# Reordering the gather stage of a spectral-mixing and expert kernel: one-hots, one gather, one spectrum load and one turn

## The chip, the cores and the metric

The kernel runs on one core of one Trainium2 chip. The metric is the device time of one execution in microseconds (us), lower is better. Before the change it is 474.11 us, the median of three runs (473.17 to 475.94).

The core has a matrix engine (TensorE, "PE" in the profile, with its weight loads as "PEld"), a vector engine (VectorE, "DVE"), an activation engine (ScalarE, "ACT"), GpSimd ("POOL") and a queue engine (SyncE, "SP"). DMA transfers are issued by SP, ACT and POOL and run beside them. Each engine works through its own list of instructions in order and waits on semaphores for the others.

## The reference

Two steps. The first mixes each of 8 sequences of 2496 rows and 256 channels by multiplying its spectrum with a filter:

```python
X = np.fft.rfft(x, axis=1)
Y = X * (filt_r + 1j * filt_i)[None, :, :]
y = np.fft.irfft(Y, n=x.shape[1], axis=1)
```

The second treats the 19968 rows of `y` as tokens of a mixture of 8 experts with 80 places each. A token goes to its best expert; an expert that has more than 80 tokens keeps those with the largest gate; all other rows of the output are zero:

```python
logits = x @ w_gate
expert_idx = np.argmax(logits, axis=1)
gate_w = softmax(logits)[np.arange(N), expert_idx]
for e in range(E):
    tok_idx = the (at most capacity) tokens of e with the largest gate_w
    h = np.maximum(x[tok_idx] @ w1[e], 0.0)
    out[tok_idx] = gate_w[tok_idx, None] * (h @ w2[e])
```

Only 640 of the 19968 rows are needed after the choice, so the kernel never transforms back a whole sequence. It keeps the filtered spectra, computes the logits from them, chooses the rows, and transforms back only the chosen rows.

## The kernel before, in words

All instructions stand in an order written by hand (`manual_schedule`, from L782). The framework adds the waits on semaphores that the data needs; it moves nothing.

**Main loop (L853 to L896).** It runs over 80 pairs (sequence b, slice u) and two more turns of the loop. For each pair TensorE does a part of the forward transform (`stage1`, `transpose1`, `stage2`), VectorE multiplies by the filter (L339), GpSimd combines the products (L345), and `turn(b, u)` (L349) brings the result back into row order with four matrix products (L354). `turn` lags two behind, so the last one, `turn(7, 9)`, stands at loop value 81. ScalarE copies its result out, and every second turn it stores a piece of the spectrum `yf[b]` to memory. The table `early` (L836) hangs the choice of rows for the first three sequences (the early round, `pick_...` with round 0) between the turns of the loop. `pick_full(0, 0, NE)` (L683) is a check of that round that feeds only a flag for a rarely needed second path; it reads the PSUM tile `misc`.

**Row gathers and tiles.** For each sequence t there is a tile of up to 128 chosen rows. `fetch(t)` (L465) issues on GpSimd an indirect DMA that gathers 128 rows of 2560 numbers (10 KB each, 1.3 MB in all) from a table of inverse-transform coefficients, by the row numbers in `idxb[:, t]`. Two tiles share a buffer `gts`. `spectrum(t)` (L473) loads the filtered spectrum of sequence t, 2560 KB, on SP's queue; tiles 0 and 1 find it in SBUF already, the others have three buffers in turn (`ypool` twice, `st["yx"]` for t = 2 and 5). `turn_rows(t, g)` (L481) transposes a fifth of the gathered rows (TensorE L485, ScalarE copy L489 into `wt`). `add_rows(t, g)` (L491) multiplies it with the spectrum (L496). The result of a tile goes to `y_sel` in memory.

The list `work` (L901 to L907) holds these two steps in order, with the transposes two steps ahead of the products. Tiles 0 to 2 are one group and tiles 3 to 7 the next. `go(n)` (L910) emits the next n steps. After the last step of tile t, `go` emits `spectrum(t + 3)`; so spectrum 5 follows tile 2. After the last transposes of tile 3 it emits `fetch(6)` and `fetch(7)`.

**The late round (L946 to L975).** Between the steps of tiles 0 to 2 the rows of sequences 3 to 7 are chosen. `pick_slots(0)` makes the first slot of each partition. `pick_rows(1, NE, B, 5)` and part 6 (L666 to L681) make the row numbers `idxb` with small products and four VectorE operations, and `fetch(3)` follows (NE is 3). `pick_slots(1)` makes a table `eval` on GpSimd (L743). `fetch(4)` follows. `pick_slots(3)` makes the one-hots `eplc` of the slots on VectorE (L736). `pick_slots(2)` joins the two tables on TensorE (L750) after tile 2 and yields the indices of the experts' tokens. Then `gather_gates` issues eight small gathers on GpSimd (L223), `fetch(5)` follows, and tiles 3 to 7 run. `mark` is a tile of one number, written once near the start (L816) by a GpSimd copy of one loaded element; the copy makes GpSimd wait for that load.

**Experts (L977 to the end).** Gathers of the experts' rows from `y_sel`, two layers for each of eight experts, and scatters of the results.

Of the kernel before, what the change touches and what calls it, by code (L numbers as in the profile page):

```python
# [13 lines left out]
F32 = mybir.dt.float32  # L14
# [9 lines left out]
B, S, C = 8, 2496, 256  # L24
# [3 lines left out]
NU = NS // 2  # L28
# [53 lines left out]
def kernel(  # L82
# [11 lines left out]
    nc = tc.nc  # L94
# [13 lines left out]
    consts = ctx.enter_context(tc.tile_pool(name="consts", bufs=1))  # L108
# [70 lines left out]
    NE, NY, NO = 3, 2, 3  # L179
    yf = {b: dpool.tile([128, NS, C], F32, name=f"yf_{b}") for b in range(B)}  # L180
# [51 lines left out]
    with ExitStack() as actx:  # L232
        bctx = ExitStack()

        def pool(name, bufs, space=None, within=actx):
            kw = {} if space is None else {"space": space}
            return within.enter_context(tc.tile_pool(name=name, bufs=bufs, **kw))
# [9 lines left out]
        tpool = pool("tables", 1, within=bctx)  # L247
# [25 lines left out]
        def sign_filter(v):  # L273
            f = fst[:, v]
            for i in range(2):
                nc.scalar.activation(out=f[:, 2 + i, :], in_=f[:, 2 + i, :], func=AF.Copy,
                                     scale=fsig[:, 2 * v + i:2 * v + i + 1])
# [185 lines left out]
        wts, gts, ybs, pos = {}, {}, {}, {}  # L463

        def fetch(t):  # L465
            if t % 2 == 0:
                gts[t // 2] = t1pool.tile([128, 2, NS * 128], F32, name=f"gts_{t}", tag="t1")
            nc.gpsimd.indirect_dma_start(
                out=gts[t // 2][:, t % 2, :], out_offset=None, in_=rows[:, :],
                in_offset=bass.IndirectOffsetOnAxis(ap=idxb[:, t:t + 1], axis=0),  # L470
                bounds_check=S - 1, oob_is_err=False)

        def spectrum(t):  # L473
            p = ypool if t % NE < NE - 1 else st["yx"]
            ybs[t] = p.tile([128, NS, C], F32, name=f"yb_{t}", tag="ys")
            nc.sync.dma_start(out=ybs[t], in_=yf[t])

        def weights(e, p, tag, queue=nc.sync):
            load_weights(e, p.tile([128, 2 * NFC * C], F32, name=f"w_{e}", tag=tag), queue)
# [28 lines left out]
        def pt(shape, dt, name, rnd):  # L508
            return sp.tile(shape, dt, name=f"{name}_{rnd}", tag=name)
# [173 lines left out]
        def pick_full(rnd, b0, nb):  # L683
            if rnd == 0:
                nc.vector.tensor_scalar(out=viol[:, 4:5], in0=st["rcnt"][:], scalar1=float(K0),
                                        scalar2=None, op0=AL.is_gt)
            vb = pt([128, B], F32, "vb", rnd)
            nc.vector.tensor_scalar(
                out=vb[:, b0:nb], in0=st["poff"][:, 1, b0:nb], scalar1=128.0, scalar2=None,
                op0=AL.is_gt, op1=AL.add, accum_out=viol[:, 2 + 3 * (1 - rnd):3 + 3 * (1 - rnd)])  # L690
# [91 lines left out]
        with tc.manual_schedule():  # L782
# [29 lines left out]
                nc.gpsimd.memset(t[:], 0.0)  # L812
            nc.gpsimd.tensor_copy(out=gi[:, 0, E:E + 128], in_=ident[:])
            nc.gpsimd.tensor_copy(out=gi[:, 1, 0:128], in_=ident[:])
            mark = tpool.tile([1, 1], F32, name="mark")
            nc.gpsimd.tensor_copy(out=mark[:], in_=st["x", 0, NCH - 1][0:1, 0, 0:1])  # L816
            load_filter(1, 0)
            nc.gpsimd.dma_start(out=gi[:, 0, 0:E], in_=moe_w_gate[0:128, :])
# [11 lines left out]
            for v in range(LEAD):  # L830
# [8 lines left out]
                     71: [lambda: pick_misc(0), lambda: pick_tau(0), lambda: pick_kept(0, 0, NE)],  # L839
                     72: [lambda: pick_sums(0, 0, NE), lambda: pick_codes(0, 0, NE)],  # L840
                     73: [lambda: pick_fields(0), lambda: pick_rows(0, 0, NE, 0),
                          lambda: pick_rows(0, 0, NE, 1), lambda: pick_full(0, 0, NE)],
                     74: [lambda: pick_rows(0, 0, NE, 2), lambda: pick_rows(0, 0, NE, 3)],
                     75: [lambda: pick_rows(0, 0, NE, 4)],
                     76: [lambda: pick_rows(0, 0, NE, 5), lambda: pick_rows(0, 0, NE, 6),
                          lambda: fetch(0)],
                     79: [lambda: fetch(1)]}
            tops = [lambda i=i: pick_top(0, i, n0, 128) for i in range(n0)]
            third = -(-n0 // 3)
            early[68] += tops[:third]  # L850
# [2 lines left out]
            for v in range(B * NU + LATE):  # L853
                b, u = divmod(v, NU)
                if b < B:
                    stage2(b, u)
                    if v + 2 < NU:
                        if v % 2 == 1:
                            sign_filter(v // 2 + 1)
                        turn_filter(v // 2 + 1, v % 2)  # L860
                    if v < 4:
                        load_filter(3 + v // 2, v % 2)
                    elif v == 4:
                        nc.gpsimd.dma_start(out=e_t, in_=e_dram.ap())
                        nc.gpsimd.dma_start(out=wi_t, in_=wi_dram.ap())
                    w = v + LEAD
                    if w < B * NU:
                        transpose1(*divmod(w, NU))
                    put_s1()
                    if u == 3:  # L870
                        put_s1()
                    if b > 0:
                        put_zeros(1)
                if v >= LATE:
                    turn(*divmod(v - LATE, NU))
                if b > 0 and u == LATE:
                    logits(b - 1, 0)
                if b > 0 and b % 2 == 0:
                    if u == LATE + 1:
                        logits(b - 1, 1)  # L880
                    if b < 6 and u in (4, 5, 6, 7, 8, 9):
                        gating(b // 2 - 1, u - 4)
                        if u == 9:
                            gating(b // 2 - 1, 6)
                    elif b == 6 and u in (4, 5):
                        gating(2, 2 * u - 8)
                        gating(2, 2 * u - 7)
                    elif b == 6 and u in (6, 7):
                        gating(2, u - 2)
                        if u == 7:  # L890
                            gating(2, 6)
                for act in early.pop(v, []):
                    act()
                if v == B * NU:
                    turn_rows(0, 0)
                    turn_rows(0, 1)  # L896
            assert not (xs or s1 or early)
# [12 lines left out]
            def go(n):  # L910
                for kind, t, g in work[:n]:
                    if kind == "t":
                        turn_rows(t, g)
                        if g == NS // SG - 1 and t == NE:
                            fetch(6)
                            fetch(7)
                    else:
                        add_rows(t, g)
                        if g < NS // SG - 1:
                            continue  # L920
                        if t + 3 < B:
                            spectrum(t + 3)
                        if t == 4:
                            weights(0, wpool, "w")
                            weights(1, wpool, "w")
                del work[:n]
# [30 lines left out]
            for part in range(5):  # L957
                pick_rows(1, NE, B, part)
            pick_slots(0)
            go(FG[4])  # L960
            pick_rows(1, NE, B, 5)
            pick_rows(1, NE, B, 6)
            fetch(NE)
            pick_slots(1)
            fetch(NE + 1)
            pick_slots(3)
            go(FG[5])
            pick_full(1, NE, B)
            pick_bad()
# [583 lines left out]
```

## Time and profile before

| what | us |
|---|---|
| median of three runs | 474.11 |
| profiled execution, whole | 481.94 |
| profiled execution, span from first to last instruction | 480.1 |
| last matrix products of the main loop (L354) start | 299.31 |
| tile 0 starts (L485) | 298.38 |
| tile 3 starts | 338.00 |
| tile 4 starts | 348.76 |
| last product of tile 7 (L496) | about 396.2 |
| experts' first product (L1115) | 400.08 |

Durations and starts are of the profiled execution, counted from its first instruction. A line of the timeline gives the start, the duration, the engine, the source line and operation, what is written and read, how many instructions are merged, and in brackets how long the engine had been idle and what ended that. A matrix product of 4-byte numbers shows as two records for each weight load and product, so four products are "x8". The waits view lists the idle time of an engine by what ended it: total, number of times, longest. The view of stretches lists for each engine its busy time and number of instructions, in the order PE, PEld, DVE, ACT, POOL, then the granted TensorE clock (1.00 is full), the DMA share and the GB/s moved.

### The profile page before, as it was taken

Reading aid. Unit: us, or ns where it says so; the run is one execution under the profiler, and the core shown is the slowest. Engines: PE = TensorE matmul, PEld = TensorE weight load, DVE = VectorE, ACT = ScalarE, POOL = GpSimd, SP = SyncE. Lnnn points to the kernel's source line nnn. Section 1 sums busy time; section 2 is a strip of 40 time slices with the busy share of each in tenths; the row PEclk is TensorE's granted clock in tenths of the full one; section 3 lists DMA queues with packets and bytes.
Section 4 is the critical chain, followed back from the end, with each engine's and each line's share of the span. In section 5 each row is a group of like instructions: output and inputs, shape, how many; then the busy total and the mean of one; then the engine's idle time right before and its main releaser. Section 6 shows DMA issues by size and latency. Waiting matters only on the chain. (4 is left out here: it accounts for less than half of the span.)

```text
span 480.1 us, 8658 instructions
## 1 busy us (share of the span) xinstructions
PE 442.1 (92%) x3372; PEld 416.0 (87%) x3372; DVE 187.9 (39%) x562; ACT 222.4 (46%) x364; POOL 176.6 (37%) x244
## 2 busy tenths in 40 slices
PE   5869999999999999999999987999889996999990
PEld 5769999999999999999999887888778886888870
DVE  2135553554664455655546995484110000011100
ACT  3835667666766666676667443322123220011110
POOL 7486434443543443444435446103620010211210
PEclk9979999999999999999999999999899996699996
DMA  7995467888778878788961326888779999155000
GB/s 215 279 293 167 151 192 218 246 262 251 250 247 254 268 271 248 203 265 280 401 238 47 132 89 213 311 338 324 283 268 383 379 389 349 53 181 173 20 18 11
DMA packets 38324, 109.95 MB, mean 229 GB/s; under 512 B 4667, under 2 KB 14202, under 8 KB 36760
## 3 DMA queue, kind: packets, MB, share of 16 engines
q1 hardware_dynamic: 26224, 73.26, 46.5%
q10 hardware_dynamic: 8642, 24.19, 13.1%
q0 software_dynamic: 3408, 11.86, 7.4%
q8 instruction: 29, 0.48, 0.4%
q14 instruction: 21, 0.17, 0.1%
HBM read 68.97 MB, written 43.20 MB: 234 GB/s over the span
## 5 line engine op out<-in xcount | busy, mean ns | idle before, releaser
L345 POOL TENSOR_TENSOR p<-p,p 128x256 f32<-128x256 f32 x160 | 114.0, 735 | 139.0 <-DVE p L339 97.2
L339 DVE TENSOR_TENSOR p<-pb,ft 128x512 f32<-128x512 f32 x160 | 102.3, 681 | 13.1 <-PE pb L331 10.7
L306 PE MATMUL pa<-wf_t,x 117*128 117x120 f32 x704 | 93.3, 280 | 6.6 <-DMA x<-in_x_dram 6.6
L312 ACT COPY t<-pa 128x480 f32<-128x480 f32 x88 | 87.0, 1000 | 26.4 <-PE pa L306 26.0
L306 PEld LDWEIGHTS pa<-wf_t,x 117*128 117x128 f32 x704 | 87.4, 197 | 6.9 <-DMA x<-in_x_dram 5.8
L354 PE MATMUL py<-gi,p 128*128 128x136 f32 x640 | 88.1, 280 | 1.3 <-POOL p L345 1.3
L331 PE MATMUL pb<-d_t,t 128*128 128x128 f32 x640 | 86.1, 278 | 0.9 <-DVE p L339 0.8
L354 PEld LDWEIGHTS py<-gi,p 128*128 128x128 f32 x640 | 79.8, 190 | 1.9 <-POOL p L345 1.9
L331 PEld LDWEIGHTS pb<-d_t,t 128*128 128x128 f32 x640 | 78.9, 193 | 1.7 <-DVE p L339 1.0
L322 ACT COPY t<-pt 128x512 f32<-128x512 f32 x80 | 46.9, 586 | 69.4 <-PE pt L320 64.8
L496 PE MATMUL po<-yb,wt 128*128 128x256 f32 x240 | 57.3, 383 | 2.0 <-ACT wt L489 2.0
L496 PEld LDWEIGHTS po<-yb,wt 128*128 128x128 f32 x240 | 43.8, 192 | 7.4 <-ACT wt L489 2.5
L320 PE MATMUL pt<-ident,t 128*128 128x128 f32 x320 | 48.5, 274 | 0.0
L489 ACT COPY wt<-pw 128x512 f32<-128x512 f32 x40 | 23.3, 586 | 54.1 <-PE pw L485 52.4
L374 DVE COPY z<-py 128x16 f32<-128x16 f32 x60 | 11.2, 186 | 91.9 <-ACT ysp L369 57.9
L320 PEld LDWEIGHTS pt<-ident,t 128*128 128x128 f32 x320 | 38.1, 143 | 0.0
L369 ACT COPY ysp<-py 128x512 f32<-128x512 f32 x60 | 35.4, 590 | 0.0
L1129 PEld LDWEIGHTS ph<-xs,w 128*128 128x128 f32 x256 | 32.9, 209 | 1.7 <-DVE xs L1120 1.2
L1129 PE MATMUL ph<-xs,w 128*128 128x80 f32 x256 | 33.1, 293 | 0.8 <-DVE xs L1120 0.8
L1144 PE MATMUL po<-w,hT 128*80 128x256 f32 x128 | 31.2, 402 | 0.0
L485 PE MATMUL pw<-ident,gts 128*128 128x128 f32 x160 | 24.7, 281 | 4.6 <-DMA gts<-rows_tbl,idxb 4.6
L1099 POOL DMA_INDIRECT xg<-y_sel,idxg x8 | 7.7, 962 | 55.9 <-ACT wt L489 40.3
(195 smaller groups left out, 315.7 us busy)
## 6 DMA issues: line engine op xcount, KB each, us to landing
out_dram<-zero_t SPq DMA_DIRECT2D x64, 312.0 KB
x<-in_x_dram SPq DMA_DIRECT2D x40, 468.0 KB
yf<-ysp ACTq DMA_DIRECT2D x30, 512.0 KB
yb<-yf SPq DMA_DIRECT2D x6, 2560.0 KB
w<-in_moe_w_dram SPq DMA_DIRECT2D x14, 1024.0 KB
yf<-ys ACTq DMA_DIRECT2D x10, 512.0 KB
w<-in_moe_w_dram ACTq DMA_DIRECT2D x2, 1024.0 KB
x<-in_x_dram SPq DMA_DIRECT2D x8, 234.0 KB
```

What stands on the lines that cost most here:

```text
L306: nc.tensor.matmul(out=ps[:, i, :, 2 * NS * cb:2 * NS * cb + 2 * NS], lhsT=xt[0:NJ * N1, (2 * k + i) % JC, 128 * cb:128 * cb + 128], rhs=w ...
L312: nc.scalar.copy(out=t1[:, 2 * k - h:2 * k - h + 2], in_=ps[:])
L320: nc.tensor.transpose(ps[:, i, cb, :], t1[:, a:a + 2, :].rearrange("p r n -> p (r n)"), ident[:])
L322: nc.scalar.copy(out=t2[:].rearrange("p i c -> p (i c)"), in_=ps[:].rearrange("p i c q -> p (i c q)"))
L331: nc.tensor.matmul(out=ps[:, cb, i], rhs=d_t[:, 2 * u + i, :], start=True, stop=True, lhsT=t2[:, i, 128 * cb:128 * cb + 128])
L339: nc.vector.tensor_tensor(out=pt, in0=ps[:].rearrange("p c s r q -> p (c s) r q"), in1=f.unsqueeze(2).to_broadcast([128, 2 * NDB, 2, NQ]), ...
L345: nc.gpsimd.tensor_tensor(out=yt[:, :, r, :], in0=yt[:, :, r, :], in1=pr[1][:, :, 1 - r, :], op=op)
L354: nc.tensor.matmul(out=ps[:, i, ZW * cb:ZW * cb + ZW], rhs=gi[:, cb, :], lhsT=yt[:, 2 * cb + i].rearrange("p r q -> p (r q)"), start=True, ...
L369: nc.scalar.copy(out=dst, in_=ps[:, :, E:E + C])
L496: nc.tensor.matmul(pos[t][:, 0, 0:C], lhsT=wts[t, g // 2][:, g % 2, i, :], rhs=ybs[t][:, s, :], start=(s == 0), stop=(s == NS - 1))
L1129: nc.tensor.matmul(ph[:, fc // 4, fc % 4, 0:cap], lhsT=self.w1s[e][:, k, 128 * fc:128 * fc + 128], rhs=xs[:, k, :], start=(k == 0), stop=( ...
L1144: nc.tensor.matmul(po[0:cap, :], lhsT=hT[:, fc, :], rhs=self.w2s[e][:, fc, :], start=(fc == 0), stop=(fc == NFC - 1))
```

## The change

Five edits, all in the order of instructions:

1. The first two `turn_rows` of tile 0 move from loop value 80 to 81, behind `turn(7, 9)`. TensorE now does the last turn and then the transposes, and ScalarE copies the turn's result out, issues its store, and then copies the transposes.
2. `pick_full(0, 0, NE)` moves from loop value 73 to 81. On VectorE its two operations now stand behind the last turn's addition.
3. `pick_slots(3)` moves ahead of parts 5 and 6 of `pick_rows`. On VectorE the one-hots `eplc` stand before the four operations that make `idxb`.
4. A GpSimd copy of one element of the gathered rows of tile 3 into `mark` stands before `fetch(4)`. GpSimd waits there until gather 3 has landed. The tile `mark` moves to a pool that lives to the end.
5. `spectrum(5)` is no longer issued by SP after tile 2. ScalarE issues it after its copy of the second transposes of tile 3. SP's list is one transfer shorter and otherwise the same.

```diff
-        def spectrum(t):
+        def spectrum(t, queue=nc.sync):
...
-            nc.sync.dma_start(out=ybs[t], in_=yf[t])
+            queue.dma_start(out=ybs[t], in_=yf[t])
...
-            mark = tpool.tile([1, 1], F32, name="mark")
+            mark = consts.tile([1, 1], F32, name="mark")
...
                      73: [lambda: pick_fields(0), lambda: pick_rows(0, 0, NE, 0),
-                          lambda: pick_rows(0, 0, NE, 1), lambda: pick_full(0, 0, NE)],
+                          lambda: pick_rows(0, 0, NE, 1)],
...
-                     79: [lambda: fetch(1)]}
+                     79: [lambda: fetch(1)],
+                     81: [lambda: pick_full(0, 0, NE)]}
...
-                if v == B * NU:
+                if v == B * NU + 1:
                     turn_rows(0, 0)
                     turn_rows(0, 1)
...
+                        if (t, g) == (NE, 1):
+                            spectrum(NE + 2, nc.scalar)
                     else:
                         add_rows(t, g)
...
-                        if t + 3 < B:
+                        if t + 3 < B and t != NE - 1:
                             spectrum(t + 3)
...
             pick_slots(0)
+            pick_slots(3)
             go(FG[4])
             pick_rows(1, NE, B, 5)
             pick_rows(1, NE, B, 6)
             fetch(NE)
             pick_slots(1)
+            nc.gpsimd.tensor_copy(out=mark[:], in_=gts[NE // 2][0:1, NE % 2, 0:1])
             fetch(NE + 1)
-            pick_slots(3)
             go(FG[5])
```

## The prediction

> **What bounds the kernel now.** I read the page's busy times first, then the waits of TensorE, then the timeline around each wait, then stretches of 1 us for clock and DMA.
>
> ```profile
> PE 442.1 (92%) x3372; PEld 416.0 (87%) x3372; DVE 187.9 (39%) x562; ACT 222.4 (46%) x364; POOL 176.6 (37%) x244
> ```
>
> TensorE works 92% of the span, so time is won only where it stands still. The waits view, filtered to TensorE (us in total, times, longest), says where:
>
> ```profile
> PE pa L306 <- DMA x<-in_x_dram: 6.6, 3, 5.8
> PE pf L284 <- ACT fst L276: 4.8, 4, 3.5
> PE pw L485 <- DMA gts<-rows_tbl,idxb: 4.6, 2, 2.4
> PE px L1115 <- DMA xg<-y_sel,idxg: 3.9, 1, 3.9
> PE po L496 <- ACT wt L489: 2.0, 1, 2.0
> ```
>
> The first two are the start of the kernel, which the change leaves alone. The third is two waits for gathered rows: 2.40 us before tile 0 and 2.25 us before tile 3. These the change is about. The timeline (start, duration, engine, line, idle time before and its releaser) at tile 0:
>
> ```profile
> 298.38 1.09 PE L485 MATMUL pw<-ident,gts 128*128 128x128 f32 x8 [2.40 <-DMA gts<-rows_tbl,idxb]
> 299.08 1.07 ACT L489 COPY wt<-pw 128x512 f32<-128x512 f32 x2 [2.39 <-PE pw L485]
> 299.21 1.00 PEld L354 LDWEIGHTS py<-gi,p 128*128 128x128 f32 x8
> 299.31 1.09 PE L354 MATMUL py<-gi,p 128*128 128x136 f32 x8
> 300.13 1.60 PEld L496 LDWEIGHTS po<-ys,wt 128*128 128x128 f32 x8
> ```
>
> The last turn (L354) sits behind the gather's wait although its input was ready: GpSimd's last products end at 291.95 + 4.15 = 296.10. At tile 3:
>
> ```profile
> 327.49 1.49 DVE L736 TENSOR_TENSOR eplc<-slot,iota 128x1280 bf16<-128x1280 f32 x1
> 327.85 2.00 POOL L468 DMA_INDIRECT gts<-rows_tbl,idxb  x1 [18.03 <-DVE idxb L681]
> ...
> 331.52 1.03 POOL L468 DMA_INDIRECT gts<-rows_tbl,idxb  x1 [0.16 <-issue]
> ```
>
> ```profile
> 335.19 29.34 SPq L476 DMA_DIRECT2D yb<-yf  x3
> ...
> 338.00 1.94 PE L485 MATMUL pw<-ident,gts 128*128 128x128 f32 x8 [2.25 <-DMA gts<-rows_tbl,idxb]
> ```
>
> Gather 3 is issued while VectorE builds the slots' one-hots (2.00 us instead of 1.03), gather 4 follows at 331.52, spectrum 5 at 335.19, and tile 3 starts at 338.00. The stretches of 1 us (busy time by engine, granted clock, DMA share, GB/s) show that the wait also costs clock:
>
> ```profile
> 336.00:337.00 1.00, 0.00 (x0) 0.00 (x0) 0.89 (x7) 0.00 (x0) 0.00 (x0) 1.00 1.08 338
> 337.00:338.00 1.00, 0.00 (x1) 0.03 (x1) 0.83 (x7) 0.00 (x0) 0.16 (x1) 0.76 0.71 276
> 338.00:339.00 1.00, 1.00 (x5) 1.00 (x6) 0.53 (x2) 0.00 (x0) 0.83 (x1) 0.50 1.21 451
> 340.00:341.00 1.00, 1.00 (x3) 0.82 (x4) 0.00 (x0) 0.56 (x1) 0.69 (x2) 0.54 1.19 507
> ```
>
> **What the Trainium skill says.** (1) "TensorE: Matmul & The Clock Gate", Part 1 (What's actually happening): activity is judged in free-running windows of 3.413 us and an idle one halves the clock. The trace agrees: the shares put the drop at 337.52 and the release at 340.92, and the other cold stretch, 398.96 to 416.02, lies 18 and 23 such windows after 337.52. The 2.40 us wait at tile 0 straddles two windows and cost no clock. (2) "DMA: Bandwidth & Descriptors", Queues, rings and completion order: each DMA engine alternates between queues packet by packet. The DMA view agrees for 357 to 366: 4 to 9 gather packets per us beside 9 to 21 of spectrum loads, and gather 7, issued by 353.21, trickles until 367. (3) The same page, Issuing engines are not separate DMA queues: another issuing engine brings no bandwidth. (4) "GPSIMD Engine Reference", 1. Specifications: GpSimd shares its SBUF interfaces with VectorE operations of two SBUF inputs. The 2.00 against 1.03 us agrees.
>
> **The change part by part.** Sums are in the profiled execution: span 480.1, whole run 481.94, against a median of 474.11 without profiling.
>
> *Last turn ahead of tile 0.* It runs from 296.15 to 297.3, inside the wait. Then tile 0's first product waits for ScalarE's copy of the first bank, 299.08 + 0.59 = 299.67, where it started its weights at 300.13. Gain 0.40. The turn's ScalarE copies and store also come first; they end by 298.4, before the copy at 299.08, so they cost nothing. If the gather came 1 us earlier, they would delay that copy by about 0.3.
>
> *Violation checks of the early round moved behind the last turn.* L685 and L688 leave VectorE at 282.69 to 282.83, where it is busy 2.00 of 2.00 us and TensorE waits for it. At most 0.14, and I take 0.14. In the new place VectorE is idle until 304.40.
>
> Both shift all that follows by 0.54: TensorE has no wait from 302 to 335.7.
>
> *One-hots (L736) before the row indices.* They fall into VectorE's idle time, 325.15 to 326.81 (1.66 us for 1.49), so the indices are not later; if they overran, the gather would be later by the overrun, 0 to 0.3. The gather's issue should shrink from 2.00 to about 1.0. But its packets begin only at 332.2, as spectrum 4 (issued 324.3) drains at 332 to 333; a gather issued to an idle machine starts about 1.4 after its issue (291.93 to 293.3). So it was held 0.9 by the spectrum, and an earlier issue gains 0 to 0.5. I take 0.2.
>
> *Gather 4 held until gather 3 has landed (the copy to mark); spectrum 5 after tile 3's second copy.* Gather 3 took 332.2 to 338.0 = 5.8. Gather 0, nearly alone, took about 293.3 to 298.38 = 5.1. Gain 0.7, between 0 (one ring serves gather 3 first anyway) and 1.2. With the 0.2 above: 0.9, ends 0 and 1.7. TensorE then idles 1.35 instead of 2.25. That is below the 1.84 us of one window that passed at tile 0, so I expect no cold window; it cost (1.94 - 1.09) of transposes, hidden but for 0.4, and 2.55 - 1.89 = 0.66 of products: 1.0 to 1.1. I take 1.0.
>
> Now the price. Call T tile 3's start, 336.56. GpSimd waits until T, copies (0.18), passes semaphores (0.3) and issues gather 4 (1.03): done at T + 1.55, not 332.55; packets from T + 2.9. Behind the copy stand the eight gate gathers (first at 337.84 before, now about 338.4), then gathers 5 to 7. Gather 5 is issued at about 348.5 instead of 347.91 and is needed at 361.85: no cost. Spectrum 5 is issued on ScalarE's queue after the second copy, at T + 1.8 at full clock (298.38 to 300.15 at tile 0), packets from T + 2.9 as well. Its 0.33 us stands before tile 3's third copy, which waits for TensorE anyway; it is needed only at 364. SP's later loads keep their order. So gather 4 and spectrum 5 start together. Alone, gather 4 lands at T + 8.0; if they alternate to the end, 1.31 + 2.62 MB at 0.4 MB per us is 9.8 us, and it lands at T + 13. Tile 4's first transposes stood at 348.76, T + 10.76, and at full clock T + 9.7. Hence a new wait of 0 to 3.3. I take 0.9 (landing at T + 10.6), because a part of the gather that the engines have taken up passes before they alternate: at 355 to 357 gathers still moved 0.31 and 0.28 MB per us beside a new spectrum.
>
> From tile 4 on nothing changes its order. Sum: -0.54 - 0.9 - 1.0 + 0.9 = -1.5, so 480.4 for the run of 481.94, 0.997. That gives 472.6. With all ends at their best it is -3.4, at their worst +2.8.
>
> An open point is the wait of 2.0 after tile 4's first transposes: ScalarE, VectorE and GpSimd all resume at 350.7 to 350.9 on TensorE's signal, though TensorE's records run on to 349.4. No view names its cause. I leave it in place; if it goes, 2.0 more is won, and if it stays, the new wait may lie inside it.
>
> **Rivals.**
> - *The wait moves to tile 4 and outweighs the rest.* Alternation to the end makes gather 4 land at T + 13 or later; TensorE idles 3.3 and more, which fills a clock window and costs some 1.1 to 2 again. -2.4 + 3.3 + 2 = +2.9: 477.0. For it: gather 7's trickle. Against: 0.31 and 0.28 MB per us at the meeting. It decides from a wait of 2.4 on (no gain), 4.8 for slower by 0.5%. Chance 0.2.
> - *The gather is no faster alone.* Then only the turn and the checks count, and the cold window stays or not: -0.5 to -0.9, 473.4. For it: one ring serves gather 3 ahead of gather 4. Chance 0.25.
> - *The new wait is none and the unexplained 2.0 goes too:* -2.4 - 2.0 = -4.4, 469.8. For it: DMA was nearly idle from 346 to 349, so tile 4 has slack. Chance 0.2.
> - My forecast, -1.5: chance 0.35.
>
> **How the numbers follow.** About 0.5% (2.4 us) is what a measurement of this kernel can tell from no change. Faster by more: the third rival and the lower third of the forecast, whose own range is 471 to 474.5: 0.34. Slower by more: most of the first rival, 0.17. Between: 0.49. The range 469.5 to 477 reaches into both outer cases and leaves out their far ends.
>
> **What would show it.** The turn (L354) starting by 296.2 and the products near 299.6; gather 3's issue near 1.0 us; tile 3's wait near 1.4 and clock 1.00 after it; then the wait of tile 4's transposes for gts, which decides. I am wrong if that wait exceeds 2.4, if tile 3's stays above 2, or if the clock falls elsewhere, since the windows run free: the cold stretch at 399 to 416 alone holds about 7 us.

## The result and the profile after

The changed kernel took 477.97 us (median of 20 runs, 472.63 to 483.65), the kernel before 474.50 beside it (20 runs, 470.89 to 477.71). The quotient of the medians is 1.0073. The comparison gives a ratio of 1.0151, 95% interval 1.0105 to 1.0196; its ratios leave out executions more than 1.5% above the fastest of their kernel, 6 of the 20 here and 54 of the 59 of the kernel before in the set of e1 to e4, so in that set the medians are the better guide. Either way the change made the kernel slower. The profiled execution of the changed kernel took 483.33 us whole (span 481.5), against 481.94 (480.1) before. So the profiles differ by 1.4 us and the medians by 3.5. The profiled execution before is 4.2 us above the longest of the 20 runs, so it may hold a wait that they do not have; the experiments come back to this.

The waits of TensorE in the changed kernel (us in total, times, longest):

```profile
PE pw L485 <- DMA gts<-rows_tbl,idxb: 7.4, 3, 3.8
PE po L496 <- ACT wt L489: 0.5, 2, 0.2
```

The wait for gathered rows was 4.6 us in two pieces; it is 7.4 in three, and the new piece is the longest, 3.8. The 2.0 us wait for ScalarE's copy, which the forecast had left open, is gone.

The timeline of the changed kernel at tile 0:

```profile
294.61 1.19 PE L354 MATMUL py<-gi,p 128*128 128x136 f32 x8 [0.16 <-POOL p L345]
297.02 1.09 PE L485 MATMUL pw<-ident,gts 128*128 128x128 f32 x8 [1.22 <-DMA gts<-rows_tbl,idxb]
298.35 1.99 PE L496 MATMUL po<-ys,wt 128*128 128x256 f32 x8 [0.24 <-ACT wt L489]
```

The last turn now runs inside the gather's wait. From the first transposes to the first product it is 298.35 - 297.02 = 1.33 us, where it was 300.24 - 298.38 = 1.86.

The timeline of the changed kernel from the one-hots to tile 4, each line with start, duration, engine and, in brackets, the idle time before it and its releaser:

```profile
323.41 1.49 DVE L736 TENSOR_TENSOR eplc<-slot,iota 128x1280 bf16<-128x1280 f32 x1
326.06 0.99 POOL L468 DMA_INDIRECT gts<-rows_tbl,idxb  x1 [18.04 <-DVE idxb L681]
336.28 0.18 POOL L969 COPY mark<-gts 1x1 f32<-1x1 f32 x1 [7.72 <-DMA gts<-rows_tbl,idxb]
336.36 1.06 PE L485 MATMUL pw<-ident,gts 128*128 128x128 f32 x8 [2.40 <-DMA gts<-rows_tbl,idxb]
337.15 1.05 POOL L468 DMA_INDIRECT gts<-rows_tbl,idxb  x1 [0.69 <-PE pw L485]
337.62 0.33 ACTq L476 DMA_DIRECT2D yb<-yf  x1
...
350.05 1.09 PE L485 MATMUL pw<-ident,gts 128*128 128x128 f32 x4 [3.79 <-DMA gts<-rows_tbl,idxb]
350.18 0.94 POOL L223 DMA_INDIRECT gate<-gates,idxt  x1 [3.09 <-DMA gts<-rows_tbl,idxb]
350.94 3.62 PE L496 MATMUL po<-yb,wt 128*128 128x256 f32 x8
```

Gather 3 is issued in 0.99 us, as forecast. Tile 3 still waits 2.40 us for it. GpSimd sees it land, and gather 4 is issued from 337.15 to 338.20 instead of at 331.52. ScalarE's spectrum 5 is issued from 337.62 to 337.95, so it is out first. Tile 4's transposes wait 3.79 us, until 350.05, which is 13.7 us after T = 336.36, the start of tile 3. The products behind them take 3.62 us, where eight such products take 1.89 at full clock. The stretches show the clock (the number after the five engines; then DMA share and GB/s):

```profile
342.00:346.00 4.00, 4.00 (x24) 3.44 (x22) 1.28 (x4) 1.17 (x2) 2.92 (x4) 1.00 0.94 399
346.00:350.00 4.00, 0.27 (x2) 0.00 (x0) 0.00 (x0) 0.00 (x0) 0.95 (x1) 0.85 0.43 167
350.00:354.00 4.00, 3.95 (x12) 3.35 (x13) 0.00 (x0) 0.59 (x1) 2.96 (x3) 0.50 0.22 38
```

TensorE is full until 346, stands still until 350 and then runs four microseconds at half clock.

The DMA view of the changed kernel shows what went ahead of gather 4. The first line is from 338 to 342, the two below are from 342 to 346 (packets, MB, share of the engines' time; q10 carries the spectrum and q0 the gathers):

```profile
q10 hardware_dynamic: 58, 1.19, 91.1%
...
q10 hardware_dynamic: 61, 1.19, 69.1%
q0 software_dynamic: 94, 0.40, 24.6%
```

For four microseconds only the spectrum moves. Gather 4 appears at 342, and then gets 0.40 MB where the spectrum gets 1.19.

### The profile page after: what moved, and what is told of

It is laid out like the page before. It is cut to its first block, busy times and chain, and to the rows that moved or that the text cites. A ratio compares the mean times of both kernels' runs of the same rounds, so it can differ in the third digit from the quotient of the medians.

```text
span 481.5 us, 8657 instructions
## 1 busy us (share of the span) xinstructions
PE 442.9 (92%) x3372; PEld 415.7 (86%) x3372; DVE 187.8 (39%) x562; ACT 222.5 (46%) x364; POOL 175.5 (36%) x245
## 5 line engine op out<-in xcount | busy, mean ns | idle before, releaser
L339 DVE TENSOR_TENSOR p<-pb,ft 128x512 f32<-128x512 f32 x160 | 102.3, 681 | 11.2 <-PE pb L331 11.2
L322 ACT COPY t<-pt 128x512 f32<-128x512 f32 x80 | 46.9, 586 | 67.3 <-PE pt L320 67.3
L496 PE MATMUL po<-yb,wt 128*128 128x256 f32 x240 | 58.6, 390 | 0.2 <-ACT wt L489 0.2
L496 PEld LDWEIGHTS po<-yb,wt 128*128 128x128 f32 x240 | 44.8, 196 | 5.7 <-ACT wt L489 0.5
L374 DVE COPY z<-py 128x16 f32<-128x16 f32 x60 | 11.2, 187 | 91.6 <-ACT ysp L369 57.9
L485 PEld LDWEIGHTS pw<-ident,gts 128*128 128x128 f32 x160 | 20.1, 145 | 11.4 <-issue 6.8
```

Source lines behind the costliest of these rows:

```text
L322: nc.scalar.copy(out=t2[:].rearrange("p i c -> p (i c)"), in_=ps[:].rearrange("p i c q -> p (i c q)"))
L339: nc.vector.tensor_tensor(out=pt, in0=ps[:].rearrange("p c s r q -> p (c s) r q"), in1=f.unsqueeze(2).to_broadcast([128, 2 * NDB, 2, NQ]), ...
L485: nc.tensor.transpose(ps[:, i, :], gts[t // 2][:, t % 2, 128 * s:128 * s + 128], ident[:])
L496: nc.tensor.matmul(pos[t][:, 0, 0:C], lhsT=wts[t, g // 2][:, g % 2, i, :], rhs=ybs[t][:, s, :], start=(s == 0), stop=(s == NS - 1))
```

## The experiments

For every kernel two stages are read from ScalarE's copies in the timeline. The *start stage* runs from the copy of tile 2's sum (yr) to tile 3's first copy of transposed rows (wt). The *tile stage* runs from there to the copy of tile 4's sum. In the kernel before they are 339.12 - 335.19 = 3.93 and 364.22 - 339.12 = 25.10. *Signal* is the time from the start of TensorE's product L775 to VectorE's copy of it (L777), normally 0.3. The tile stage also holds what a fall of the clock behind tile 3's start costs. Each set of runs has the kernel before beside it, and that kernel's median was not the same in all sets: 474 us in two, 480 to 481 in three. Each set ran on one chip, and the set of e1 to e4 (474) and that of p1 to e6 (480) on the same one. So kernels are compared within their set.

| kernel | median, before beside it | ratio (95%) | start stage | tile stage | signal |
|---|---|---|---|---|---|
| before, first profile | | | 3.93 | 25.10 | 3.79 |
| changed, first profile | 477.97, 474.50 | 1.0151 (1.0105 to 1.0196) | 3.62 | 28.98 | 0.31 |
| e1 no copy | 475.46, 473.96 | 1.0125 (1.0051 to 1.0198) | 3.09 | 22.27 | 0.31 |
| e2 spectrum back | 476.23, 473.96 | 1.0110 (1.0060 to 1.0160) | 3.33 | 23.88 | 0.31 |
| e3 neither | 474.11, 473.96 | 1.0015 (0.9990 to 1.0040) | 3.39 | 23.58 | 0.31 |
| e4 spectrum later | 483.45, 473.96 | 1.0194 (1.0143 to 1.0245) | 3.32 | 31.78 | 0.31 |
| p1 before | one run, 480.12 | | 4.10 | 24.94 | 3.46 |
| p2 changed | one run, 480.12 | | 3.25 | 27.71 | 0.31 |
| p3 no copy | one run, 480.12 | | 3.77 | 25.34 | 3.88 |
| e6 spectrum 4 behind | 481.28, 480.12 | 1.0030 (1.0010 to 1.0049) | 1.08 | 28.86 | 1.51 |
| e9 gates later | 477.25, 480.73 | 0.9932 (0.9907 to 0.9957) | 2.92 | 24.87 | 0.30 |
| e10 both | 475.72, 480.73 | 0.9894 (0.9868 to 0.9919) | 1.07 | 22.47 | 0.31 |
| e11 changed | 480.72, 480.73 | 0.9965 (0.9937 to 0.9993) | 2.67 | 27.88 | 0.30 |
| e12 neither | 479.44, 480.73 | 0.9974 (0.9954 to 0.9995) | 3.85 | 25.09 | 3.70 |
| e13 gather 5 first | 477.16, 481.24 | 0.9923 (0.9898 to 0.9949) | 3.48 | 22.63 | 1.89 |
| e14 gates later, gather 5 held | 477.04, 481.24 | 0.9918 (0.9893 to 0.9943) | 3.01 | 23.95 | 0.30 |
| e15 both, again | 475.25, 481.24 | 0.9891 (0.9845 to 0.9937) | 1.07 | 22.28 | 0.31 |

### The copy and the place of the spectrum

My theory after the result was that copy and spectrum together make gather 4 late. Rivals: the spectrum alone does it, or tile 4's wait is not what costs.

**e1** takes the copy out of the changed kernel:

```diff
-            nc.gpsimd.tensor_copy(out=mark[:], in_=gts[NE // 2][0:1, NE % 2, 0:1])
             fetch(NE + 1)
```

> T is the start of tile 3's first transposes. Theory A (gather 4 is late: the copy on GpSimd keeps it from being issued until gather 3 is seen, T+0.8): without the copy gather 4 is issued at about T-6, lies in the queue right behind gather 3 and lands by T+5; tile 4's transposes don't wait, the clock doesn't drop there, and tile 4's last yr comes at T+23 to T+26 instead of T+29.6. Ratio to before 0.992 to 0.999. Theory B (the spectrum that ScalarE issues at T+1.3 takes the DMA engines, and its issue holds up ScalarE's copies, whenever the gather is issued): a wait of 1 us or more stays at tile 4, ratio 1.000 to 1.010. Theory C (tile 4's wait is taken up later anyway, by the wait for the experts' first gather; the loss is elsewhere): the wait goes and the time stays at 1.007 or above.

Timeline of e1:

```profile
325.44 1.03 POOL L468 DMA_INDIRECT gts<-rows_tbl,idxb  x1 [0.16 <-issue]
332.56 1.06 PE L485 MATMUL pw<-ident,gts 128*128 128x128 f32 x8 [1.87 <-DMA gts<-rows_tbl,idxb]
333.82 0.33 ACTq L476 DMA_DIRECT2D yb<-yf  x1
...
342.31 0.60 PE L485 MATMUL pw<-ident,gts 128*128 128x128 f32 x4
```

Gather 4 is issued 7.1 us before tile 3 starts (332.56), and tile 4's transposes at 342.31 wait for nothing. The tile stage is 22.27 us instead of 28.98. So the wait goes as theory A has it. The time did not follow as far: the median is 475.46, above the expected range, with runs in two groups, 470.1 to 473.6 and 475.4 to 479.6, and this profile (470.37 whole) is of the lower one.

**e2** keeps the copy and gives spectrum 5 back to SP after tile 2:

```diff
-                        if (t, g) == (NE, 1):
-                            spectrum(NE + 2, nc.scalar)
...
-                        if t + 3 < B and t != NE - 1:
+                        if t + 3 < B:
                             spectrum(t + 3)
```

> The copy stays, spectrum 5 is issued by SyncE after tile 2 as before. Theory A: gather 4 is still issued at T+0.8, but the spectrum has started some 2 to 3 us earlier; gather 4 lands at T+9.5 to T+12 and the wait at tile 4 shrinks from 3.8 to 0 to 2 us; gather 3 meets the spectrum's packets again at its end, so T may be up to 1 us later. Ratio 0.998 to 1.005. Theory B: no wait at tile 4, ratio 0.995 to 0.999. Theory C: 1.007 or above.

Timeline of e2:

```profile
332.16 0.32 SPq L476 DMA_DIRECT2D yb<-yf  x1
334.83 1.06 PE L485 MATMUL pw<-ident,gts 128*128 128x128 f32 x8 [2.11 <-DMA gts<-rows_tbl,idxb]
335.61 1.05 POOL L468 DMA_INDIRECT gts<-rows_tbl,idxb  x1 [0.67 <-DVE diag L770]
```

Gather 4 is issued as late as in the changed kernel, 0.8 us after tile 3's start, but the spectrum has a lead of 3.45 us. Tile 4 does not wait, and the tile stage is 23.88. So lateness alone does not make the wait. The time is 2.3 us above the kernel before (476.23 and 473.96), at the upper end of what was expected. The 1.6 us of the tile stage beyond e1's 22.27 are the clock's, which falls to half in e2 behind the first transposes and not in e1 (the last three numbers are clock, DMA share and GB/s):

```profile
337.00:339.00 2.00, 2.00 (x6) 1.53 (x6) 0.00 (x0) 0.00 (x0) 1.64 (x2) 0.50 1.03 441
```

**e3** is without copy and with the spectrum by SP: both edits above. What is left of the change is the first tile's turn, the checks and the one-hots.

> Only the first tile's turn, the moved checks and the earlier one-hots are left. Theories A and B: no wait at tile 4; first tile 0.4 to 0.5 us gained, tile 3's start 1 to 1.7 us earlier than before against tile 0; ratio 0.993 to 0.999. Theory C: the loss lies in these edits, 1.005 or above.

The median, 474.11, is that of the kernel before (473.96), so the gain that was expected from these three edits (0.993 to 0.999) does not show either. The loss is in the copy and the spectrum's place: for the changed kernel it is 477.97 - 474.50 = 3.5, in another set. What each of the two costs alone is less sure. By the medians the copy costs 2.1 us (e2 against e3) and the spectrum's place 1.4 (e1 against e3), but the 22 runs of e1 spread over 9.6 us and those of e2 over 11.2, and the second difference is not clear of that. Only together do they show the wait at tile 4 in a profile. What e1 and e2 lose beyond their profiles is not in these profiles, each of which is one execution.

**e4** issues the spectrum at tile 3's last turn, so that gather 4 has the DMA engines alone:

```diff
-                        if (t, g) == (NE, 1):
+                        if (t, g) == (NE, 4):
                             spectrum(NE + 2, nc.scalar)
```

> The copy stays; spectrum 5 is issued by ScalarE at tile 3's last turn (about T+8) instead of its second (T+1.3), so that gather 4 has the DMA engines alone. Theory A, in the form that lateness and sharing make the wait together: gather 4 lands at T+6 to T+8 and tile 4 doesn't wait; the spectrum lands at T+16 to T+18, ahead of tile 5 at about T+20; ratio 0.992 to 0.999. If lateness alone made it (the gather itself takes over 9 us from its issue, alone or not): it lands at T+10 or later, a wait of 0.5 to 4 us stays, ratio 1.000 to 1.010. Theory C: 1.007 or above.

Timeline of e4:

```profile
334.96 1.05 POOL L468 DMA_INDIRECT gts<-rows_tbl,idxb  x1 [0.66 <-DVE diag L770]
343.95 0.33 ACTq L476 DMA_DIRECT2D yb<-yf  x1
346.46 1.02 POOL L468 DMA_INDIRECT gts<-rows_tbl,idxb  x1 [0.30 <-issue]
347.75 0.32 SPq L476 DMA_DIRECT2D yb<-yf  x1
362.72 1.09 PE L485 MATMUL pw<-ident,gts 128*128 128x128 f32 x4 [6.33 <-DMA gts<-rows_tbl,idxb]
```

Tile 4 does not wait: alone, gather 4's large packets are through by 341, 6 us after its issue and 7 after tile 3's start. But the wait has only moved to tile 5 and grown to 6.33. Gather 5 is issued 2.5 us after spectrum 5 and 1.3 before spectrum 6, and lands 16.3 us after its issue. The expected ratio was missed by 10 us, and the miss says most: here and in the changed kernel the gather that meets a spectrum just issued is the one that comes late, gather 5 or gather 4.

### The same kernels again

**p1**, **p2** and **p3** are the kernel before, the changed kernel and e1 again, one execution each, to see which waits belong to a kernel.

> The kernel before again, a second profiled execution, to see which of its waits belong to the kernel. If the 2.0 us wait of tile 3's fourth turn (ACT, VectorE and GpSimd all held until PE's signal) belongs to it: from the first copy of tile 3 to tile 3's yr again 14 us. If it was an accident of one execution: 12.3 to 13.2 us, and from tile 0's first copy to the experts' first transposes some 99 us instead of 101.0.

> The changed kernel again. If tile 4's wait for gather 4 belongs to it: 2 us or more again, gather 4 landing 12 to 14 us after tile 3's start, from tile 3's first copy to its yr over 14.5 us. If it was an accident: under 1 us of wait, 11.4 to 13 us.

> The kernel without the copy on GpSimd again; its first profiled execution took 470.4 us whole, its median was 475.5, and its times lie in two groups, 470 to 473 and 475 to 480. If a wait of the tile stage makes the upper group, an execution of that group shows one of 2 us or more at tile 4 or tile 5 that the first did not have, and 98 us or more from tile 0's first copy to the experts' first transposes (96.6 in the first). If the upper group is the start of the kernel or the experts, that stretch stays at 96 to 97 us.

Tile 4's wait is there again in p2 (2.06 us, tile stage 27.71). The wait that the forecast left open is there again in p1 (1.7 us), and now also in p3, which did not have it as e1. A wait of the tile stage accordingly does make part of the spread of that kernel: the tile stage is 25.34 in p3 and 22.27 in e1, and the whole stretch from tile 0's first copy to the experts' first transposes is 100.86 against 96.58. The two executions differ by 9.7 us, so more than half of it lies elsewhere.

**e11** and **e12** are the changed kernel and e3 again, timed in one set.

> The changed kernel itself, timed on the same chip as the next run. If its loss is tile 4's wait for gather 4: a ratio of 1.004 to 1.012 to before, and from tile 3's first copy to tile 4's yr 27 to 29 us (before 25.0). If the loss was of that chip or of those executions: 0.997 to 1.003.

> The kernel with only the first tile's turn, the checks and the one-hots moved, again, on the same chip as the changed kernel. If copy and spectrum together make the whole loss: 0.996 to 1.001 as in its first timing (1.0003 by the medians), and 2.5 to 5 us less than the changed kernel. If the loss lies elsewhere in the change: within 1.5 us of the changed kernel.

Timeline of e3, and below it that of e12, the same program:

```profile
345.76 0.27 PE L775 MATMUL misc<-diag,ones_bf 80*128 80x240 bf16 x1
346.07 0.47 DVE L777 TENSOR_SCALAR last<-misc,pid 128x240 f32<-128x240 f32 x1 [8.82 <-PE misc L775]
```

```profile
344.05 0.27 PE L775 MATMUL misc<-diag,ones_bf 80*128 80x240 bf16 x1
345.89 0.60 PE L485 MATMUL pw<-ident,gts 128*128 128x128 f32 x4
347.75 0.47 DVE L777 TENSOR_SCALAR last<-misc,pid 128x240 f32<-128x240 f32 x1 [12.01 <-PE pw L485]
347.76 1.07 ACT L489 COPY wt<-pw 128x512 f32<-128x512 f32 x2 [5.09 <-PE pw L485]
```

In e3 VectorE takes the product 0.31 us after it started. In e12 it gets TensorE's signal 3.70 us after, and ScalarE at the same moment, while TensorE's records go on to the next transposes at 345.89. TensorE then waits 1.9 us for ScalarE's copy. In this set the changed kernel has the median of the kernel before (480.72 and 480.73), and e12 is 1.3 us below both. That fits: the changed kernel pays tile 4's wait (3.84 in this profile), but has no late signal at this place in any of its three profiles. Where the kernel before has the late signal, the two would cancel (and the 2.5 to 5 us expected between changed kernel and e12 be missed for that reason); where e3 shows none, in the set at 474, the loss remains.

That the kernel before lacks the late signal in the sets at 474 is inferred, since no profile of it was taken there. But the inference is stronger than e3 alone. Late signals also come at the start of the kernel, where ScalarE copies a transposed block (L322). The first two lines are of the kernel before, the last two of e1:

```profile
25.54 0.60 PE L320 MATMUL pt<-ident,t 128*128 128x128 f32 x4
29.57 0.59 ACT L322 COPY t<-pt 128x512 f32<-128x512 f32 x1 [4.59 <-remote]
...
25.12 0.60 PE L320 MATMUL pt<-ident,t 128*128 128x128 f32 x4
25.76 0.59 ACT L322 COPY t<-pt 128x512 f32<-128x512 f32 x1 [1.40 <-PE pt L320]
```

ScalarE takes the block 4.03 us after the first record in one and 0.64 in the other, and was idle meanwhile in both. At this place, the third such copy, it is 1.4 to 3.4 us late in 11 of the 12 profiles of the 480 kind (the first profile before, 481.94, and p1 to p3, e6 and e9 to e15), and in all five of the two sets at 474 (the changed kernel's first, e1 to e4) it is at most 0.5 late, and that only where the clock is at half. So the two kinds of set differ in late signals as such, and what makes a set one or the other is not on record. The changed kernel itself is 2.8 us slower here than in its first set (480.72 and 477.97).

### Spectrum 4 behind gather 3

**e6** leaves the copy out and issues spectrum 4 by ScalarE after tile 2's last turn, spectrum 5 after tile 3's fourth. Against e1:

```diff
-                        if (t, g) == (NE, 1):
-                            spectrum(NE + 2, nc.scalar)
+                        if (t, g) in ((NE - 1, 4), (NE, 3)):
+                            spectrum(t + 2, nc.scalar)
...
-                        if t + 3 < B and t != NE - 1:
+                        if t + 3 < B and t + 3 not in (NE + 1, NE + 2):
                             spectrum(t + 3)
```

> No copy on GpSimd; spectrum 4 is issued by ScalarE after tile 2's last turn, behind gather 3 instead of in front of it, spectrum 5 by ScalarE after tile 3's fourth turn. Theory: gather 3 lands late because the 2.6 MB of spectrum 4 stand ahead of it (gather 3 landed 13.7 us after spectrum 4's issue whatever came after it). Then gather 3 lands by about 332 on the clock of the kernel after, tile 3 starts without a wait right behind tile 2, 2 to 2.5 us earlier, and the clock doesn't drop there; gather 4 and spectrum 4 land within 9.5 us after that. From tile 2's yr to tile 3's first copy 1 to 1.5 us instead of 3.1 to 3.9; ratio 0.988 to 0.997. Rival 1: the gather takes its 8 to 10 us from issue by its own descriptors: the wait stays at 1.5 us or more, ratio 0.997 to 1.003. Rival 2: the wait moves on, to tile 4 (spectrum 4 or gather 4 not there) or to tile 5 (gather 5 behind spectrum 5): a wait of 2 us or more there, ratio 1.000 to 1.015.

Timeline of e6:

```profile
326.99 0.98 POOL L468 DMA_INDIRECT gts<-rows_tbl,idxb  x1 [18.04 <-DVE idxb L681]
330.79 0.33 ACTq L476 DMA_DIRECT2D yb<-yf  x1
335.42 1.07 ACT L489 COPY wt<-pw 128x512 f32<-128x512 f32 x2 [0.70 <-PE pw L485]
...
344.50 0.60 PE L485 MATMUL pw<-ident,gts 128*128 128x128 f32 x4
346.66 0.60 PE L485 MATMUL pw<-ident,gts 128*128 128x128 f32 x4
351.27 0.58 ACT L489 COPY wt<-pw 128x512 f32<-128x512 f32 x1 [6.51 <-remote]
```

Tile 3's wait is gone: no line of gts waits there any more, and the start stage is 1.08 us instead of 2.67 to 4.10. So gather 3 was late because spectrum 4 stood ahead of it. But ScalarE gets tile 4's first transposes, recorded at 344.50, only at 351.27, and the tile stage is 28.86. By these records the gain was given back by late signals and not by DMA volume alone, since TensorE's records of those transposes are not late; the view names no releaser within the program ("remote"). e10, below, has the same large transfers without this wait. The second rival is right that the wait moves on, and by this reading wrong on its cause.

### The gates' gathers elsewhere

**e9** is e3 with the eight gathers of the gates (`gather_gates`, L223) behind gathers 5 to 7. **e10** is e6 with the same edit, and **e15** is e10 again in another set.

```diff
                             fetch(6)
                             fetch(7)
+                            gather_gates()
...
             pick_slots(2)
-            gather_gates()
             fetch(NE + 2)
```

> No copy on GpSimd, spectrum 5 by SyncE after tile 2; new: the eight gathers of the gates go behind gathers 5, 6 and 7 instead of in front of gather 5. Theory: the late signals from the PE at tile 3's fourth turn (2 us in two executions of the kernel before, where ScalarE, VectorE and GpSimd went on together although the records show the PE's work done) come with the gates' small packets of that stretch. Then no such wait in this kernel and from tile 3's first copy to tile 3's yr 11.4 to 13.0 us; gather 5 is issued at about T-4 and tile 5 doesn't wait; ratio to before 0.990 to 0.997. Rival: they come with the chip or with the spectrum's packets: the wait of 1.5 us or more is there again where the kernel before shows it, ratio 0.997 to 1.003.

> As the kernel with spectrum 4 behind gather 3, with the gates' gathers behind gathers 5 to 7. Theory of the gates' packets: tile 3 starts within 1.5 us of tile 2's yr as there, and the 5 to 6 us by which tile 4 was held are gone or under 2 us; from tile 2's yr to tile 3's yr 12.5 to 14.5 us instead of 18.4; ratio 0.985 to 0.994. Rival, the DMA's volume: gathers 3, 4 and 5 and spectrum 4 must all pass within some 12 us, and tile 4 still waits 2 us or more for spectrum 4 or gather 4: ratio 0.998 to 1.008.

> Spectrum 4 behind gather 3, spectrum 5 behind tile 3's fourth turn, the gates behind gathers 5 to 7, again, for its time on another chip or in other executions. Where the kernel before takes about 480 us: 0.986 to 0.993 as in its first timing; where it takes about 474 us, and so lacks the 2 us of late signals: 0.989 to 0.997 (the 2.0 to 2.8 us of tile 3's start and what goes with its clock).

Timeline of e15:

```profile
333.48 1.07 ACT L489 COPY wt<-pw 128x512 f32<-128x512 f32 x2 [0.70 <-PE pw L485]
340.72 0.27 PE L775 MATMUL misc<-diag,ones_bf 80*128 80x240 bf16 x1
341.03 0.47 DVE L777 TENSOR_SCALAR last<-misc,pid 128x240 f32<-128x240 f32 x1 [5.20 <-PE misc L775]
343.20 0.58 ACT L489 COPY wt<-pw 128x512 f32<-128x512 f32 x1 [1.65 <-PE pw L485]
...
357.57 1.97 PE L496 MATMUL po<-yb,wt 128*128 128x256 f32 x8 [1.42 <-DMA yb<-yf]
```

Tile 3 starts without a wait, the signal takes 0.31 us, tile 4's first copy follows 9.7 us after tile 3's (343.20 - 333.48), and the time is 0.9891 of before (e10: 0.9894). The medians are 5.0 us (e10) and 6.0 us (e15) below the kernel before, and e10 is as far below the changed kernel, timed in its set. What is left there is 1.42 us for a spectrum further on; I did not try to remove it. All kernels with the gates or gather 5 moved were timed in sets at 480 alone. What they gain where the kernel before takes 474 us is not known.

**e13** is e3 with gather 5 ahead of the gates, which stay in their stretch; **e14** is e9 with gather 5 held until gather 4 has landed.

```diff
             pick_slots(2)
-            gather_gates()
             fetch(NE + 2)
+            gather_gates()
```

```diff
+            nc.gpsimd.tensor_copy(out=mark[:], in_=gts[NE // 2 + 1][0:1, 0, 0:1])
             fetch(NE + 2)
```

> First tile, checks and one-hots moved, no copy, spectrum 5 by SyncE; new: gather 5 goes ahead of the gates' eight gathers, which stay where they were. If the late signals of the PE at tile 3's fourth turn come with the gates' small packets: the wait of some 2 us is there again (on a chip on which the kernel before shows it, about 480 us) and the ratio is 0.996 to 1.001. If they come with gather 5, issued there behind the gates: no wait, DVE's copy within 1 us after the product it takes, from tile 3's first copy to its yr under 13.3 us, ratio 0.990 to 0.996.

> The gates' gathers behind gathers 5 to 7, but gather 5 held until gather 4 is seen (about T+5 to T+8). If the gates' packets make the late signals: no such wait, under 13.3 us from tile 3's first copy to its yr, ratio 0.991 to 0.998. If gather 5's descriptors beside tile 3 do: a wait of 1.5 us or more, ratio 0.996 to 1.002.

With the gates moved away the signal takes 0.30 us wherever gather 5 stands (e9, e14, as in e10 and e15). With the gates in place and gather 5 ahead of them it still takes 1.89 (e13), but costs little: the tile stage is 22.63, against 22.27 in e1 without it. So neither expectation of e13 fits whole: the late signal stays with the gates, the time goes with gather 5. It is won either way (0.9923 and 0.9918).

With the gates moved the lateness is gone from that place, but it has moved with them. Timeline of e9, from the first of the gates' gathers on:

```profile
348.90 0.98 POOL L223 DMA_INDIRECT gate<-gates,idxt  x1 [0.27 <-issue]
...
354.13 0.60 PE L485 MATMUL pw<-ident,gts 128*128 128x128 f32 x4
356.18 0.58 ACT L489 COPY wt<-pw 128x512 f32<-128x512 f32 x1 [2.99 <-PE pw L485]
```

ScalarE takes these transposes 2.05 us after their start, where 0.64 is normal. It is 2.05 in e10, 1.38 in e14 and 1.37 in e15, each in the stretch to which the gates were moved. In all ten profiles that have a late signal in the tile stages it comes 7 to 14 us after the first of the gates' gathers is issued. TensorE waits for little of it in the new place (0.5 us in e9). So the gates' gathers decide where the signals are late, and with gather 5 what that costs. They are not all of the cause: at the start of the kernel the gates have no part, only other gathers that GpSimd issues (L268), and e1 to e4, with the gates in place, have no late signal anywhere. Why TensorE's signals are held back is not shown.

## Why the prediction was wrong

The forecast was -1.5 us, the result +3.5 by the medians. It took its sums from a profile of 481.94 us and carried them over to a kernel timed at 474.11. That profile has late signals, which no profile of the two sets at 474 has, so it seems to be of another kind than the runs. Its steps, in its own order:

- *Last turn ahead of tile 0, -0.40.* Right: 1.86 to 1.33 us, -0.53. The checks' -0.14 could not be told apart.
- *One-hots and gather 3 alone, -0.9.* The one-hots were hidden, and the gather's issue shrank to 0.99 us, as forecast. The gain did not come: from tile 1's yr to tile 3's start it was 338.00 - 324.35 = 13.65 us before and 336.36 - 322.57 = 13.79 after, and 13.57 in e3, where gather 4 stood right behind gather 3. The second rival, "the gather is no faster alone", holds for this step. The forecast had seen that gather 3 was held by spectrum 4, but took only 0.9 us of it as held and looked for the rest behind the gather, in gather 4 and spectrum 5. e6 shows that it stood ahead.
- *No cold clock at tile 3, -1.0.* It came in this profile (1.06 us of transposes for 1.94), but by luck and not for the reason given: the wait did not shrink (2.40 for 2.25). Of the fourteen profiles with a wait of 1.45 to 2.42 us there, the clock falls to half at tile 3 in ten, in five of them only at the end of the first eight transposes or behind them (as in e2); it stays in the changed kernel's first, e1, e11 and e13. This is the free-running window of "TensorE: Matmul & The Clock Gate", Part 1: which wait falls on a window is chance, and should have been carried as a range. The window need not be idle throughout, and the 1.84 us of idle time in one window that the forecast took for safe was not: in its own profile the window that ends with the fall at 337.52 began at 334.11, and TensorE stood still in it only from 335.75 on, 1.77 us. In the changed kernel a border of windows lies at 335.15 (four times 3.41 before the fall at 348.8) and parts the 2.40 us into halves.
- *The new wait at tile 4, +0.9.* This is the step that failed. The landing was taken as T + 10.6, on the ground that a part of the gather passes before the two transfers alternate. It was T + 13.7. The assumption that "gather 4 and spectrum 5 start together" was wrong: ScalarE's issue began at T + 1.3, not T + 1.8, while its second copy still ran (337.03 to 338.10 for the two), and was done at 337.95; GpSimd's took 1.05 us and was done at 338.20. The gather's first packets moved at 342, T + 5.6, where T + 2.9 was forecast, and it was a part of the spectrum, 1.19 MB in four microseconds, that passed first. Why so small a lead keeps the gather out for so long is not shown; in e4, where it is alone, its rows move within a microsecond of the issue's end. From 342 on the two share the engines. That is the turn-taking by packets of "DMA: Bandwidth & Descriptors", Queues, rings and completion order, but not one for one: from 342 to 346 there passed 58 whole packets of the spectrum, of 20 KB each, beside 39 rows of the gather, of 10 KB each (the other packets of the two queues are under 512 B). So the gather had a quarter of the bytes. The wait was 3.79 us (2.06 and 3.84 in other executions), and the eight products behind it lost 3.62 - 1.89 = 1.7 us to the clock.
- *The open wait of 2.0, left in place.* It went in all three profiles of the changed kernel. The third rival had that term right, and tied it to the wrong condition, a new wait of none. By the profiles of e1 to e4 it was not in the runs at 474 to begin with.

The first rival, "the wait moves to tile 4 and outweighs the rest", is what happened, at nearly its price: it put 3.3 of wait and 2 of clock, and 477.0 in all. That the total is so near is in part luck, since it counts 0.9 us of gain at the gather that did not come. It was given a chance of 0.2. What should have weighed for it is that the landing was bounded by T + 8.0 and T + 13, tile 4 stood at T + 9.7, and nothing in the profile put a gather ahead of a spectrum issued beside it; its one argument against, 0.31 and 0.28 MB per us at 355 to 357, was of a gather that was already under way.

In the set at 480 the forecast comes close (480.72 against 480.73) only, by this reading, because the new wait and the late signal that went cancel.

## What to carry to other kernels

Before a transfer is held back or moved, list everything that the DMA engines hold ahead of it and beside it: here what made a gather late was each time the large load issued before it, and moving that load behind it took the wait away (e6, e10). A small wait put on an issuing engine moves every later issue of it, here into the next large transfer, so follow each of them to its consumer. A wait in one profile may belong to that execution: look at it in a second one before it is made a base for a sum. A profiled execution 7.8 us above the median of the runs (481.94 and 474.11) was the sign of it here.

## What was not expected of the hardware

TensorE's signals can reach ScalarE, VectorE and GpSimd 1.5 to 3.9 us after the start of a product that they normally take in 0.3, all at the same moment (350.71, 350.72 and 350.91 in the kernel before), with TensorE's own records running on. At tile 3's last turn it was seen in 6 of 17 profiles, in executions of the same kernel with and without it; with the four in which it moved along with the gates' gathers, the tile stages show it in 10. At the start of the kernel it was seen in 11. All of these are profiles of the 480 kind, of which every one has a late signal at one place or the other. The five others have none at either.

The clock's halving followed the idle time in one free-running window sharply. The windows can be laid out in each trace from the moments at which its clock falls. Of those that began at full clock between 40 and 392 us, none with up to 1.67 us of idle TensorE was followed by half clock, all twelve with 2.03 us or more were, and of the twelve between 1.77 and 1.97 us six. The idle times are of TensorE's records, whose ends are modelled.

The time of one unchanged kernel differed by sets of runs, 474 against 480 to 481 us at the median, on one and the same chip too. The changed kernel was 3.5 us slower than the kernel before in one, and level with it in another (e11).
